# Turning q, k and u by DMA, masks on GpSimd too, and one written order for TensorE, in a fused attention and mixer kernel

## The chip, the cores and the metric

The kernel runs on one core of one Trainium2 chip. The metric is the time of one execution on the device in microseconds; the median of several runs is given. A core has five engines that run side by side: TensorE (PE in the profile) multiplies matrices and writes to PSUM, an accumulator memory of eight banks; VectorE (DVE) and ScalarE (ACT) read PSUM and work element by element; GpSimd (POOL) works on the main on-chip memory alone; SyncE (SP) only issues transfers. Transfers (DMAs) are issued from the queues of SP and POOL here, and 16 DMA engines carry them out.

## The reference

Inputs are q, k, v of 4 batches, 8 heads, 768 rows and 64 columns in float32. Attention keeps, for each row, the 128 latest keys and the first 4 (the "sinks"). Its result, put together over heads, is x of 768 x 512 for each batch, and a mixer follows:

```python
keep = is_sink | in_window
scores = np.where(keep, scale * q @ k.T, -1e9)
a = exp(scores - max) ; a = a / (sum(a) + 1e-09)
x = (a @ v) with the heads side by side        # 768 x 512 per batch
h = np.maximum(x.T @ w_tok1, 0.0) @ w_tok2     # over rows: 768 -> 256 -> 768
u = x + h.T
h2 = np.maximum(u @ w_ch1, 0.0) @ w_ch2        # over columns: 512 -> 1536 -> 512
return u + h2
```

## The kernel before

Heads go in pairs, four pairs to a batch: pair p belongs to batch p // 4, so there are 16. The two heads of a pair lie on the two halves of the 128 partitions once q and k are turned (columns of a head on partitions, rows along the free side), which is the form that TensorE needs for the scores.

**Loading.** Pairs 0 to 3 are loaded in float32 on SP's queue and cast to bfloat16 by an engine. Pairs 4 to 15, all v and all weights are loaded on POOL's queue with the cast in the DMA; each q or k takes two DMAs (one per head). Six buffers hold q and k of bfloat16 (`NQ`).

**Turning q and k.** `turn(p, n)` turns q or k of pairs 0 to 4 in a unit of its own. `transposed(p)` turns q and k of pairs 5 to 15: 24 transposes on TensorE into one of the two PSUM tiles that also serve the scores (`turned_bank`). Four copies (`evict`), on ACT or DVE, bring the halves of qT and kT to on-chip memory, two small ones take the sink columns of k (`sink_columns`), and a memset by DVE (`cleared`) puts zeros where the tile's next scores are not written.

**Scores.** `scores(p, g)` computes third g of a pair's scores, followed by an exp on ACT. From pair 4 on, the thirds 1 and 2 are computed by quarters: matmuls of 64 x 64 which use the four quarters of the array at a time and leave out blocks that are masked anyway. The third 0 is computed by halves, in matmuls of 64 x 128. For pairs 0 to 3 the mask is added on TensorE (`masked`), but for one third; for the others DVE multiplies the exp by a mask of ones and zeros (`mask`).

**Values and mixer.** `sink_values` and `values` multiply with v and add up in a PSUM bank for each head; DVE divides and writes x_sb. `mix_h` and `mix_u` are the mixer over rows, in two groups of 256 columns for each batch; `mix_u` ends in an add on DVE that makes u. `turned_u` turns u on TensorE for batches 1 to 3, in 48 small transposes (24 in one case); batch 0 has `transpose_u`. Then `v1` (relu(u @ w_ch1), 24 units of four matmuls for each batch) and `out_part` (24 units of three matmuls of 512 columns, six output tiles of 128 rows for each batch), an add of u on DVE and a store on SP. The last output tile of the last batch is cut into columns of 256, 128 and 128 (`out_columns`).

**PSUM.** Of the eight banks four form the two tiles for scores ("sc"), four are single banks ("mx") for all else.

**Order.** A class `Plan` runs while the program is built. It holds an estimate of when each engine is free, gives each operation to an engine, and appends it to that engine's program; on the chip each engine and each queue then runs its own list in that order, and waits where an operand isn't ready. `run` takes TensorE's units from three sources: `first` (pairs 0 to 3 and the row mixer of batch 0, in the order in which they can begin by the estimate), `main` (the column mixer) and `side` (attention and row mixer of the later batches). `MERGED` says behind how many units of `main` each unit of `side` comes. A `burst` is one unit of several pieces that use half of the array: it turns q and k of pair p + 1, computes the first third of pair p's scores and the sink values of pair p - 1; a second burst computes the two other thirds.

Of the kernel before, what the change touches and what calls it, by code (L numbers as in the profile page):

```python
# [16 lines left out]
def kernel(  # L17
# [13 lines left out]
    nc = tc.nc  # L31
# [15 lines left out]
    MERGED = (  # L47
# [5 lines left out]
    )  # L53
    NQ = 6
    MASKED_BY_PE = [(p, g) for p in range(NHP) for g in range(NT // 2) if (p, g) != (NHP - 1, 0)]
# [4 lines left out]
    att_pool = ctx.enter_context(tc.tile_pool(name="att", bufs=2))  # L60
# [3 lines left out]
    osb_pool = ctx.enter_context(tc.tile_pool(name="osb", bufs=3))  # L64

    psum = ctx.enter_context(tc.tile_pool(name="psum", bufs=1, space=bass.MemoryType.PSUM))
    TAGS = {"sc": 2, "mx": 4}

    given = {}

    sc = [psum.tile([P, 2, 2, 4, D], FP32, name=f"ps_sc{n}", tag=f"sc{n}", bufs=1) for n in range(TAGS["sc"])]

    def bank(tag, *shape, dtype=FP32, slot=None):

        n = given[tag].pop(0) if slot is None else slot
        if tag == "sc":
            return sc[n]
        return psum.tile([P, *shape], dtype, name=f"ps_{tag}", tag=f"{tag}{n}", bufs=1)
# [5 lines left out]
    def rows_of(pidx, n):  # L84

        b, hp = pairs[pidx]
        return (q, k)[n][b, 2 * hp:2 * hp + 2].rearrange("h (p j) d -> p h j d", j=NT)
# [67 lines left out]
    keep_warm(7, 0)  # L155
# [27 lines left out]
    NKB = 2  # L183
# [28 lines left out]
    x_sb = [singles.tile([P, NT, DM], BF16, name=f"x_sb{b}") for b in range(B)]  # L212
# [37 lines left out]
    class Plan:  # L250
        def __init__(self):
            self.free = {"PE": 0.0, "ACT": 0.0, "DVE": 0.0, "SP": 0.0, "POOL": 0.0}
            self.queue, self.landings = 0.0, []
            self.half = False
            self.pending = []
            self.held = {t: [()] * n for t, n in TAGS.items()}

# [9 lines left out]
        def slots(self, tag):  # L267

            free = []
            for n, readers in enumerate(self.held[tag]):  # L270
                if all(r.done is not None for r in readers):
                    free.append((max((r.done for r in readers), default=0.0), n))
            return sorted(free)

        def spare(self):
            return self.slots("mx")[0][1]

        def start_pe(self, op):
            t = self.ready(op)
            if t is None:  # L280
                return None
            for tag, banks in op.need.items():
                free = self.slots(tag)
                if len(free) < len(banks):
                    return None
                t = max(t, free[len(banks) - 1][0])
            return max(t, self.free["PE"])
# [23 lines left out]
        def commit_pe(self, op, t):  # L311
            for tag, banks in op.need.items():
                given[tag] = [n for _, n in self.slots(tag)[:len(banks)]]
                for n, readers in zip(given[tag], banks):
                    self.held[tag][n] = readers
# [6 lines left out]
        def run(self, first, main, side):  # L322

            first, main = [list(u) for u in first], list(main)
            order = [[int(n) for n in unit.split("/")] for unit in MERGED.split()]
            side, behind = [side[n] for n, _ in order], [n for _, n in order]
            placed = 0
            while any(first) or main or side or self.pending:
                o = self.other()
                tm = self.start_pe(main[0]) if main else None  # L330
                ts = self.start_pe(side[0]) if side else None
                pick = "side" if side and (not main or behind[0] <= placed) else "main"
                t = tm if pick == "main" else ts
                early = [(t, u) for u in first if u for t in [self.start_pe(u[0])] if t is not None]
                if early:
                    soonest = min([t for t, _ in early] + ([] if t is None else [t]))
                    stay = [(t, u) for t, u in early if self.half and u[0].half and t <= soonest + SWITCH]
                    te, u = next((e for e in stay + early if e[0] <= soonest + (SWITCH if e in stay else 40.0)), (None, None))
                    if u is not None and (o is None or o[0] > te):
                        self.commit_pe(u.pop(0), te)  # L340
                        continue
# [11 lines left out]
                if pick == "main":  # L353
                    placed += 1
                else:
                    behind.pop(0)
                self.commit_pe((main if pick == "main" else side).pop(0), t)
# [35 lines left out]

    QH = NT // 2

    def prepare(p):
# [21 lines left out]
        free = ([("sk", p - 2)] if p >= 2 else [], [("s", p - NKB)] if p >= NKB else [])  # L418
# [10 lines left out]
        tiles["kT", p] = kT  # L429
# [31 lines left out]
    def transposed(p):  # L461

        def run():
            ps = turned_bank(p)
            for n in range(2):
                for j in range(NT):
                    for x in range(2):
                        rows = ds(D * x, D)
                        in_order(nc.tensor.transpose(ps[:, x, n, j], bfs[p, n][rows, j], ident[rows, rows]))  # L469
                tiles["ps_" + "qk"[n], p] = [ps[:, x, n].rearrange("d j p -> d p j") for x in range(2)]  # L470

        then = [*done["qT", p], *done["kT", p], done["kTs", p]]
        then.append(cleared(p, then))
        return piece(
            350, run, [done["q_bf", p], done["k_bf", p]], {"sc": [then]}, then, [("tq", p), ("tk", p)],
        )

    def turned_bank(key):

        tiles["ps_turned", key] = bank("sc")  # L480
        t = tiles["ps_turned", key].bitcast(BF16).rearrange("d x n b c -> d x n (b c)")[:, :, :, 2 * D:8 * D]
        return t.rearrange("d x n (j p) -> d x n j p", j=NT)

    def cleared(key, readers):

        op = Op(
            {"DVE": 400.0}, lambda e: in_order(nc.vector.memset(tiles["ps_turned", key][0:D, :, :, 3], 0.0)), readers,
        )
        op.urgent = 2
        return op  # L490
# [22 lines left out]
    def scores(p, g):  # L513
# [28 lines left out]
        def run():  # L542
            if ("pT", p) not in tiles:
                tiles["pT", p] = pt_pool.tile([P, 2, NT, 2, P], BF16, name="pT")
            if not by_pe:
                tiles["ps_s", p, g] = bank("sc")
            (by_quarters if quarters else by_halves)(tiles["ps_s", p, g])
# [4 lines left out]
        def exp(e):  # L552
            in_order(nc.scalar.activation(  # L553
# [4 lines left out]
        def mask(e):  # L558
            pt = part(tiles["pT", p][:, :, ds(2 * g, 2)])
# [15 lines left out]
    def score_sinks(p):  # L575


        def run():
            pT_sink = pt_pool.tile([P, (NT - 2) * P], BF16, name="pT_sink")
            tiles["ps_sk", p] = bank("mx", (NT - 2) * P)  # L580
            for n in (p - 1, p):
                tiles["pT_sink", n] = pT_sink
# [8 lines left out]
        def exp(e):  # L591
            in_order(nc.scalar.activation(tiles["pT_sink", p], tiles["ps_sk", p], AF.Exp, scale=scale))
# [5 lines left out]
        return piece(225, run, deps, {"mx": [[x]]}, [x], [("sk", p - 1), ("sk", p)])  # L598

    def pv(p, half):  # L600
# [30 lines left out]
        n = Op({"DVE": 550.0}, norm, [r])  # L631
# [10 lines left out]
    def sink_values(p):  # L642
# [15 lines left out]
        for i in range(2):  # L658
# [11 lines left out]
            done["x", p, i] = Op({"DVE": 550.0}, norm, [done["r", p, i]])  # L670
# [19 lines left out]
    def sink_rows(p):  # L690
        def both(e):
            for i in range(2):
                r = D * i + ODD * (p % 2)
                copy(e, v_sinks[p % NHP][r:r + n_sink, i], vs[p][0:n_sink, i, 0])

        done["vs", p] = Op({"ACT": 440.0, "DVE": 400.0}, both, [done["v", p], done["pv", p - NHP]])
# [18 lines left out]

    def uT_half(b, ct, half):
        uT = tiles["mix", b][2]
        return uT.rearrange("c (k t p) -> c k t p", k=NC, t=NT)[:, ct, half * QH:(half + 1) * QH]

    def mix_h(b, g, t0, n):  # L720
        c0, cn = group(b, g)

        def run():
            if ("mix", b) not in tiles:
                tiles["mix", b] = (
                    mix_pool.tile([P, NTOK, DM], BF16, name="h1T"),
                    mix_pool.tile([P, NT * DM], BF16, name="u_sb"),
                    mix_pool.tile([P, NC * S], BF16, name="uT"),
                )
# [7 lines left out]

        w = n * cn
        op = Op(
            {"ACT": 190.0 + 0.78 * w, "DVE": 150.0 + 1.05 * w},  # L740
            lambda e: relu(e, tiles["mix", b][0][:, t0:t0 + n, c0:c0 + cn], tiles["ps_h", b, g, t0]),
# [367 lines left out]
```

## Time and profile before

| what | value |
|---|---|
| median of 3 runs | 207.51 us (207.47 to 207.58) |
| span of the profiled execution | 206.7 us |
| granted TensorE clock | 1.000 |
| v1 matmuls, 384 columns | 384, 66.3 us busy |
| output matmuls, 512 columns | 276 seen, 64.9 us busy |
| exp on ACT, 128 x 1024 | 32, 1,027 ns each |
| issue on POOL of a DMA of q or k | 48, about 823 ns each |
| store of an output tile, 256 KB, issue to landing | 2.0 us (median) |
| load of q, 96 KB, issue to landing | 7.0 us (median) |

The span is the time from the first to the last instruction of one profiled execution; the runs' times are of unprofiled ones and lie 0.8 us above it. Lengths of matmuls overlap, as a matmul begins before the one before it has left the array, so their sum is not the time that they take. "Idle before" of an engine tells what ended its wait. The chain follows the execution back from its end, at each step to what was waited for.

### The profile page before, as it was taken

To read this page: it belongs to the slowest core of one execution; us is meant where nothing else is said; L and a number is where in the kernel's file an instruction comes from. 1 tells how busy PE (TensorE), PEld (TensorE's weight loads), DVE (VectorE), ACT (ScalarE), POOL (GpSimd) and SP (SyncE) were. 2 spreads that over 40 slices of the span, in tenths; PEclk is the share of its full clock that TensorE was granted. 3 is DMA by queue.
4 is the path that set the end of the run, shared out by engine and by line. 5 is a ranking of instruction groups with operands and counts; after the bars stand their busy time and mean duration, and the time that the engine had idled before them with its cause. 6 is when DMAs were issued, how large, how long until landed. Compare 5 with 4: busy or idle time off the path is not lost.

```text
span 206.7 us, 5560 instructions
## 1 busy us (share of the span) xinstructions
PE 199.5 (97%) x2377; PEld 119.8 (58%) x2377; DVE 114.8 (56%) x263; ACT 119.0 (58%) x225; POOL 67.3 (33%) x86
## 2 busy tenths in 40 slices
PE   6798999999999999999999999999999999999994
PEld 2344795565565665666665555656655555565443
DVE  4687545649767777566675775784357252000222
ACT  4599666878744744888676443977562105773000
POOL 6099687696499984441000000000000000000000
PEclk9999999999999999999999999999999999999999
DMA  6999999999999999596001121100001212000223
GB/s 197 293 228 137 165 190 176 170 160 197 175 184 175 186 190 182 79 107 43 0 3 54 51 101 55 54 0 3 0 3 51 101 54 101 0 3 0 101 101 102
DMA packets 73223, 21.58 MB, mean 104 GB/s; under 512 B 63216, under 2 KB 70256, under 8 KB 73200
## 3 DMA queue, kind: packets, MB, share of 16 engines
q0 software_dynamic: 67232, 11.80, 72.7%
q1 hardware_dynamic: 5968, 9.45, 12.8%
q8 instruction: 18, 0.29, 0.6%
q14 instruction: 5, 0.04, 0.1%
HBM read 26.75 MB, written 6.29 MB: 160 GB/s over the span
## 4 chain that ended last, share of the span: by engine, by line
PE 86%; DMA 7%; DVE 2%; POOL 1%; ACT 1%; issue 0%; SPq 0%; POOLq 0%
PE ps_mx L121 78%; PE ps_sc L121 4%; DMA w_tok<-in_moe_w_tok_dram 4%; DMA v_sink_f<-in_v_dram 3%; PE ps_sc L469 2%; PE ps_mx L439 1%; POOL v_aug L114 1%; PE ps_mx L124 1%; SPq L200 0%; DVE u_sb L765 0%; POOL v_sink L130 0%; DVE qT L130 0%; PE ps_mx L451 0%; DVE kT L130 0%; DVE x_sb L664 0%
## 5 line engine op out<-in xcount | busy, mean ns | idle before, releaser
L121 PE MATMUL ps_mx<-w_ch,v1T 128*128 128x512 bf16 (+2 forms) x312 | 67.5, 363 | 0.0
L121 PE MATMUL ps_mx<-uT,w_ch 128*128 128x384 bf16 x384 | 66.3, 326 | 0.3 <-DVE recip L661 0.3
L553 ACT ACTIVATE pT<-ps_sc 128x1024 bf16<-128x1024 f32 (+1 forms) x48 | 44.5, 955 | 12.1 <-PE ps_sc L121 11.8
L121 PEld LDWEIGHTS <-w_ch 128*128 128x128 bf16 x384 | 36.2, 98 | 24.5 <-issue 1.5
L134 ACT ACTIVATE v1T<-ps_mx 128x384 bf16<-128x384 f32 x74 | 36.1, 493 | 16.5 <-PE ps_mx L121 16.0
L121 PEld LDWEIGHTS <-v1T 128*128 128x128 bf16 x312 | 28.2, 98 | 26.9 <-issue 0.7
L938 DVE TENSOR_TENSOR o_sb<-ps_mx,u_sb 128x512 f32<-128x512 f32 x23 | 15.9, 690 | 37.2 <-PE ps_mx L121 37.2
L121 PEld LDWEIGHTS <-w_tok 128*128 128x128 bf16 x192 | 18.4, 98 | 7.0 <-DMA w_tok<-in_moe_w_tok_dram 1.2
L106 POOL DMA_DIRECT2D q_bf<-in_q_dram x24 | 19.7, 824 | 4.6 <-DMA w_ch<-in_moe_w_ch_dram 2.0
L106 POOL DMA_DIRECT2D k_bf<-in_k_dram x24 | 19.6, 822 | 4.5 <-DMA w_ch<-in_moe_w_ch_dram 2.2
L114 POOL DMA_DIRECT2D v_aug<-in_v_dram x16 | 16.5, 1030 | 10.6 <-PE ps_mx L121 5.6
L765 DVE TENSOR_TENSOR u_sb<-ps_mx,x_sb 128x512 bf16<-128x512 f32 x20 | 13.2, 687 | 9.0 <-PE ps_mx L121 8.9
L136 DVE TENSOR_SCALAR v1T<-ps_mx 128x384 bf16<-128x384 f32 x22 | 12.2, 558 | 7.8 <-PE ps_mx L121 7.0
L121 PE MATMUL ps_mx<-v_aug,pT 128*128 128x65 bf16 x352 | 15.5, 194 | 0.0
L121 PEld LDWEIGHTS <-pT 128*128 128x128 bf16 x352 | 13.8, 97 | 2.7 <-issue 0.6
L121 PE MATMUL ps_sc<-qT,kT 64*64 64x192 bf16 (+3 forms) x288 | 15.0, 252 | 0.0
L561 DVE TENSOR_TENSOR pT<-pT,mask_main 128x1024 bf16<-128x1024 bf16 (+1 forms) x24 | 13.9, 618 | 0.0
L121 PE MATMUL ps_mx<-h1T,w_tok 128*128 128x256 bf16 x96 | 13.4, 272 | 0.0
L121 PE MATMUL ps_mx<-x_sb,w_tok 128*128 128x256 bf16 x96 | 12.0, 273 | 0.9 <-DMA w_tok<-in_moe_w_tok_dram 0.9
L130 DVE COPY qT<-ps_sc 128x384 bf16<-128x384 bf16 x11 | 6.1, 558 | 11.8 <-ACT qT L128 11.8
L664 DVE TENSOR_TENSOR x_sb<-ps_mx,recip 128x384 bf16<-128x384 f32 x22 | 11.6, 549 | 0.1
L128 ACT ACTIVATE kT<-ps_sc 128x384 bf16<-128x384 bf16 x16 | 7.3, 489 | 6.9 <-DVE qT L130 6.9
(74 smaller groups left out, 166.3 us busy)
## 6 DMA issues: line engine op xcount, KB each, us to landing
out_dram<-o_sb SPq DMA_DIRECT2D x23, 256.0 KB, 2.0
v_aug<-in_v_dram POOLq DMA_DIRECT2D x16, 192.0 KB, 7.0
w_ch<-in_moe_w_ch_dram POOLq DMA_DIRECT2D x8, 384.0 KB, 8.9
q_bf<-in_q_dram POOLq DMA_DIRECT2D x24, 96.0 KB, 7.0
k_bf<-in_k_dram POOLq DMA_DIRECT2D x24, 96.0 KB, 6.0
q_f<-in_q_dram SPq DMA_DIRECT2D x4, 384.0 KB, 5.9
k_f<-in_k_dram SPq DMA_DIRECT2D x4, 384.0 KB, 6.2
w_tok<-in_moe_w_tok_dram POOLq DMA_DIRECT2D x2, 384.0 KB, 8.5
```

What stands on the lines that cost most here:

```text
L106: in_order(nc.gpsimd.dma_start(out=out[:, h], in_=rows[:, h]))
L114: in_order(nc.gpsimd.dma_start(out=v_aug.rearrange("p i t d -> p (i t) d")[:, :, 0:D], in_=v[b].rearrange("h s d -> (h s) d")[2 * hp * S:2 ...
L121: in_order(nc.tensor.matmul(*args, skip_group_check=True, **kwargs))
L128: in_order(nc.scalar.activation(out, in_, AF.Copy))
L130: in_order({"DVE": nc.vector, "POOL": nc.gpsimd}[e].tensor_copy(out=out, in_=in_))
L134: in_order(nc.scalar.activation(out, in_, AF.Relu))
L136: in_order(nc.vector.tensor_scalar_max(out=out, in0=in_, scalar1=0.0))
L553: in_order(nc.scalar.activation(part(tiles["pT", p][:, :, ds(2 * g, 2)]), of_keys(tiles["ps_s", p, g])[:, :, 0:width(g)], AF.Exp, scale=scale,
L561: in_order(nc.vector.tensor_tensor(out=pt, in0=pt, in1=m, op=ALU.mult))
L664: in_order(nc.vector.tensor_tensor(out=x_sb[b][:, :, ds((2 * hp + i) * D, D)], in0=tiles["ps_o", p, i][:, :, 0:D], in1=tiles["recip", p, i ...
L765: in_order(nc.vector.tensor_tensor(out=u_part(b, g, s0, n), in0=tiles["ps_u", b, g, s0], in1=x_sb[b][:, s0:s0 + n, c0:c0 + cn], op=ALU.add,))
L938: in_order(nc.vector.tensor_tensor(out=o_sb.rearrange("p (g c) -> p g c", g=2), in1=u_rows(b, st), in0=tiles["ps_out", b, st].rearrange("p ...
```

## The change

In short: (1) q and k of pairs 8 to 15 (`BY_DMA = 2 * NHP`) are turned by DMAs on SP's queue, on-chip memory to on-chip memory, as one DMA for each q and k; their rows are loaded in another assignment to partitions (row j x 128 + p on partition p), and the sink columns of k are copied from kT. `kTb` and the pool of qT have three buffers in place of two. (2) u of batches 2 and 3 is turned by one DMA behind each `mix_u` (three for a group, six for a batch). (3) Copies of sink rows of v to `v_sinks` are DMAs on SP where they were copies of ACT. (4) The thirds 1 and 2 may have their mask from POOL, in four selects, where the plan gives it that. (5) `transposed`, now for pairs 5 to 7, takes two single banks; the memset `cleared` goes. (6) When the units of the first pairs and of batch 0's row mixer are all placed, the second tile of the scores also serves as two single banks; in that tile the thirds 1 and 2 are computed by halves, in the first tile by quarters. (7) `ORDERED` is the whole order of TensorE's units, by streams: s, m, t, o, h, g for the first pairs and batch 0, a for attention, k for the row mixer, c for v1 and x for output units of three matmuls. (8) The last output tile is whole; o_sb has two buffers for three, x_sb two for four. (9) Eight subtractions of blocks of w_ch2 on DVE are put in (`weight_sums`); they serve another way of multiplying (`products`), which `BY_SEVEN = ()` switches off.

```diff
-    MERGED = (
...
+    ORDERED = (
+        "t0-1 m0 s0 m1 s1 t2 m2 t3 s2 m3 s3 o0 m4 t4 s4 m5 t5 o1 s5 t6 m6 o2 s6 o3 m7 t7 s7 m8 s8 o4 m9 s9-10 g0 "
+        "s11 g1 m10 o5-6 s12 o7 g2 o8 a0 g3 a1 h0-1 g4-5 h2-4 g6 h5-6 a2 c0-2 g7 h7 c3 a3 c4-9 a4 c10-12 a5 "
+        "c13-14 a6-7 c15-18 a8-10 x0 c19-20 k0 a11 x1 k1 x2 c21-23 k2-3 x3 a12-14 x4-6 a15 x7-10 a16 x11 a17-18 "
+        "x12-14 k4 x15-16 k5-7 x17-19 a19 x20-23 c24 a20 c25-26 a21-22 c27-28 a23 c29-31 a24 c32-35 a25-26 c36-37 "
+        "a27 c38-39 k8 c40-41 a28 x24 a29 c42-43 a30 c44 k9 a31 c45 k10 x25 c46 k11 c47 x26 a32 x27 a33-34 x28 "
+        "a35 x29-30 k12 x31 a36 k13 a37-38 x32-33 k14 a39 x34-44 a40 x45-46 k15 x47 a41 c48-49 a42 c50 a43 c51-53 "
+        "k16 c54-55 k17 c56 a44-45 c57 a46 c58-59 k18 c60-62 a47 x48 c63-64 k19 c65 a48 c66 a49 c67-71 k20 x49-50 "
+        "k21 x51-55 k22-23 x56-67 c72 x68 c73 x69-70 c74 x71 c75-86 x72 c87-95 x73-95"
     )
+    SC_LATE = 1
+    BY_SEVEN = ()
+    BY_DMA = 2 * NHP
...
+        if pidx >= BY_DMA:
+            return rows.rearrange("h (j p) d -> p h j d", p=P)
...
+                    for n in range(2 * SC_LATE if self.late else 2 * NSC, 2 * NSC + NMX):
...
+        if p >= BY_DMA:
+            def turn(e, n):
+                if not n:
+                    tiles["qT", p] = att_pool.tile([P, S], BF16, name="qT2")
+                in_order(nc.sync.dma_start_transpose(
+                    out=(kT if n else tiles["qT", p]).rearrange("c (t p) -> c t p", t=NT),
+                    in_=bfs[p, n].rearrange("p t h d -> p (t h d)"),
+                ))
+
+            for n, name in enumerate(("q", "k")):
+                op = Op({"SP": 1500.0}, lambda e, n=n: turn(e, n), [done[name + "_bf", p], *free[n]], lag=4000.0)
...
+            done["kTs", p] = Op(
+                {"POOL": 300.0, "DVE": 300.0}, sinks_of, done["kT", p] + [("sk", p - NHP)],
+            )
...
+            (by_quarters if quarters and tiles["ps_s", p, g] is sc[0] else by_halves)(tiles["ps_s", p, g])
...
+            if e == "POOL":
+                for n in range(2):
+                    nk = 2 if n == 0 or g < NT // 2 - 1 else 1
+                    for i in range(2):
+                        pt = tiles["pT", p][:, i, 2 * g:2 * g + nk, n]
+                        in_order(nc.gpsimd.affine_select(
+                            out=pt, in_=pt, compare_op=ALU.is_ge, fill=0.0, base=-n,
+                            pattern=[[0, nk], [1 - 2 * n, P]], channel_multiplier=2 * n - 1,
+                        ))
+                return
...
+            if g:
+                then[-1].cost["POOL"] = 1700.0 if g < NT // 2 - 1 else 1450.0
...
-                copy(e, v_sinks[p % NHP][r:r + n_sink, i], vs[p][0:n_sink, i, 0])
+                in_order(nc.sync.dma_start(out=v_sinks[p % NHP][r:r + n_sink, i], in_=vs[p][0:n_sink, i, 0]))
...
+        if pairs[BY_DMA][0] <= b:
+            def turn(e):
+                in_order(nc.sync.dma_start_transpose(
+                    out=tiles["mix", b][2].rearrange("c (g t p) -> c g t p", g=2, p=P)[:, g, 2 * s0:2 * (s0 + n)],
+                    in_=u_part(b, g, s0, n).rearrange("p t c -> p (t c)"),
+                ))
+
+            then.append(Op({"SP": 1500.0}, turn, [op], lag=4000.0))
...
-            if b == B - 1 and st == NT - 1:
-                units += [out_columns(st, 0, 2 * P), out_columns(st, 2 * P, P), out_columns(st, 3 * P, P)]
-                continue
...
+                o_sb = tiles["o_sb", b, st] = osb_pool.tile([P, DM], FP32, name="o_sb", bufs=2)
...
+        for name, out, in0, in1, of in (
+            ("T1", t1, b12, lambda: b11, ()), ("T2", t2, b22, t1, ("T1",)),
+            ("T3", t3, b22, lambda: b12, ()), ("T4", t4, b21, t2, ("T2",)),
+        ):
...
+            queue((name, c), Op({"DVE": 85.0 + 0.53 * k * DM // 2}, run, loaded + [done[n, c] for n in of]))
...
+    for c in range(2):
+        weight_sums(c)
```

More of the change, by code (lines that the diff above doesn't have):

```diff
@@ L320, in commit_pe, with run @@
             self.pending.extend(op.then)
[L322 to L328, printed above, removed]
-                o = self.other()
[L330 to L340, printed above, removed]
-                        continue
+        def run(self, units, early):
+            early = len(early)
+            units = list(units)
+            while units or self.pending:
+                self.late = early == 0
+                o = self.other()
+                t = self.start_pe(units[0][1]) if units else None
                 if o is not None and (t is None or o[0] <= t):
@@ L392, in piece, with joined, run @@
         return op
+    def joined(*units):
+        def run():
+            for u in units:
+                u.fn()
+        need = {}
+        for u in units:
+            for f in u.then:
+                f.deps = [d for d in f.deps if d is not u]
+            for tag, banks in u.need.items():
+                need.setdefault(tag, []).extend(banks)
+        return unit(
+            sum(u.size for u in units), run, [d for u in units for d in u.deps], need,
+            [t for u in units for t in u.then], half=units[0].half,
+        )
     QH = NT // 2
@@ L463, in run @@
         def run():
-            ps = turned_bank(p)
+            ps = [bank("mx", 2, NT, D, dtype=BF16) for _ in range(2)]
             for n in range(2):
```

453 lines of the change are left out of this document (293 added, 160 removed), and 5 rows, old and new, of the table MERGED.

## The prediction

> **What bounds the kernel now.** I read the page's busy rows and slices first, then the chain that ended last, then a table of stages, and last the timeline around the steps that the change touches.
>
> ```profile
> PE 199.5 (97%) x2377; PEld 119.8 (58%) x2377; DVE 114.8 (56%) x263; ACT 119.0 (58%) x225; POOL 67.3 (33%) x86
> ...
> DMA  6999999999999999596001121100001212000223
> ...
> PE 86%; DMA 7%; DVE 2%; POOL 1%; ACT 1%; issue 0%; SPq 0%; POOLq 0%
> ```
>
> TensorE (PE) is busy nearly throughout and makes 86% of the chain; VectorE (DVE) and ScalarE (ACT) have over 40% free. The DMA engines are full up to slice 18 (93 us) and nearly idle later. Busy alone is no proof for a pipelined engine, so the stages (span; then PE, PEld, DVE, ACT, POOL busy; clock; DMA):
>
> ```profile
> 21.00:62.00 41.00, 40.55 (x509) 27.00 (x508) 26.01 (x61) 29.32 (x57) 30.50 (x38) 1.00 1.90 178
> 62.00:98.00 36.00, 35.96 (x556) 22.28 (x554) 24.98 (x57) 24.02 (x49) 22.51 (x27) 1.00 1.68 138
> 98.00:140.00 42.00, 42.00 (x587) 25.32 (x585) 29.44 (x62) 26.16 (x53) 0.00 (x0) 1.00 0.11 39
> 140.00:170.00 30.00, 30.00 (x268) 18.03 (x269) 15.04 (x29) 11.37 (x21) 0.00 (x0) 1.00 0.10 37
> 170.00:204.00 34.00, 33.76 (x250) 19.04 (x249) 5.72 (x11) 12.60 (x25) 0.00 (x0) 1.00 0.15 57
> ```
>
> From 21 us on PE idles about 0.5 us (0.45 in the first row, 0.04 in the second; the 0.24 of the last row is its end at 203.8). So from there the span is a sum of PE work: a PE instruction removed shortens it, and work on other engines costs nothing until PE waits for it. Before 21 us the chain is loads and casts; the first pairs keep their instructions, and the written order there (turn, mask, scores) is nearly that of the trace, so I put this stage at no change.
>
> **The change, part by part.** Its turns on PE are seen here (start, length, engine and line, shape):
>
> ```profile
> 103.00 0.35 PE L469 MATMUL ps_sc<-ident,q_bf 64*128 64x64 bf16 x12
> ...
> 103.18 0.34 PE L469 MATMUL ps_sc<-ident,k_bf 64*128 64x64 bf16 x12
> ...
> 103.36 0.38 PE L121 MATMUL ps_sc<-qT,kT 64*128 64x256 bf16 x4
> ...
> 103.58 0.28 PE L121 MATMUL ps_mx<-v_sink,pT_sink 64*128 64x65 bf16 x8
> ...
> 107.81 0.49 PE L121 MATMUL ps_sc<-qT,kT 64*64 64x192 bf16 x16
> ...
> 108.12 0.60 PE L439 MATMUL ps_mx<-ident,u_sb 64*64 64x64 bf16 x48
> ...
> 108.65 2.76 PE L121 MATMUL ps_mx<-w_ch,v1T 128*128 128x512 bf16 x12
> ```
>
> Lengths overlap in the pipeline, so I take start to start. **Turns of q and k**: 103.36 - 103.00 = 0.36 us a pair, eight pairs, -2.9 us. The chain gives each 0.46 by its modelled ends, -3.7; starts decide, so -2.9, with -3.7 kept for the range. **Turns of u**, four pieces (two batches, two groups): the chain has 0.44, 0.44, 0.35 and 0.51, together 1.74; by starts the first is 108.65 - 108.12 = 0.53. I take -1.8. Together -4.7.
>
> **Scores by halves.** In the second PSUM tile of the scores the later two thirds are now computed by halves. Four matmuls of 256 columns take 103.58 - 103.36 = 0.22, and the 16 by quarters 108.12 - 107.81 = 0.31. Both thirds by halves would be 0.22 + 0.75 x 0.22 = 0.385, so +0.075 for both; as the burst needs both tiles at once, one third changes: +0.04 in 12 pairs, +0.5 us, between 0.2 and 0.9.
>
> **The tail.** The last output tile is again one of 512 columns. Its PE time is equal (6,144 columns either way). Its add takes 690 ns (the 128x512 row) in place of the 0.29 of the chain's last line, +0.4; its 256 KB store lands in 2.0 us, the 64 KB one has no landing row (128 KB: 1.7), 0 to +0.3. I take +0.5.
>
> **Evictions and memsets that go.** Per pair four copies of 128x384 (489 ns on ACT, 558 on DVE), a memset of 272 ns, two v_sink copies of 253 ns; these were hidden under PE and their removal saves nothing. The same cover hides what DVE gains: eight subtractions for sums of w_ch2, which nothing reads here, of 128x768 like the 553 ns mask row: 4.4 us near 50 to 60 us, with DVE at 26 of 41 us. Without cover each costs 0.55.
>
> **The transposes on SP.** Nothing in the trace is one. 192 KB each for q and k, 128 KB each for u. Nearest rows: 256 KB stores land in 2.0 us, and the 96 KB q loads of the crowded stage in 7.0. For q and k both lie under cover: pair 8's last load is issued at 48.2 and lands some 6 us later (k_bf's row), near 54; its scores follow pair 9's turn at 69.9. That is 15 us for two transposes, 4 to 14 us. Pair 15 is loaded by 96 and needed after 139. For u the tightest place in the written order is k15 to c54: seven units x and c of 0.65 us (eight matmuls of 384 columns take 1.29 from 104.48 to 105.77, a unit has four), two of values of 0.35 (22 matmuls for both from 103.79 to 104.48), a burst of 0.5 (the 0.31 above and its sinks) and a mix_h of 1.3 (12 matmuls of 256 columns, half of a 0.22 pair each), together 7.0 us; behind u's eviction (0.69) a transpose of 2.0 fits, one of 7.0 misses by about 1 us, in one batch. That stage has a DMA share of 0.11, so it is nearest to the 2.0. I take 0 for the transposes, at most +2.
>
> **What queues behind them on SP**: the stores and the small v_sink copies (two a pair). o_sb has two buffers for three, so an add waits for the store two tiles back, holding a PSUM bank of PE. Two tiles of 12 matmuls are 5.2 us; add, issue and landing take 0.69 + 0.33 + 2.0, so 2.2 us of delay on SP is free. **On POOL**, masks queue among load issues (0.82 us each); the loads run 15 us ahead. A mask in four pieces of 256 columns, by the POOL selects of 128 columns (290 ns) and 512 (638), is some 1.6 us against DVE's 0.69; the exp pair (1.03 + 0.81) and this fit into the shortest cover (a15 to a17: five units of 0.65 and a burst of 0.5, 3.75 us) with little to spare. For all new waits I take +0.4, between -0.5 (the idle time now there) and +2.
>
> **Sum**: -4.7 + 0.5 + 0.5 + 0.4 = -3.3 us. Span 206.7 becomes 203.4. The shown median, 207.51, lies 0.8 above the span; with that, **204.2 us**. Its own range: the low ends (-5.4, +0.2, +0.4, -0.5) give 202.2, the high ends (-4.6, +0.9, +0.8, +2) give 206.6.
>
> **Rivals.** (a) *SP becomes the bound* (slower). If a transpose among the loads holds SP's queue until it lands, at the 7.0 us of a q load, a pair costs SP 14 us plus 1 for copies and stores. From 54 us, pairs 8, 9, 10 are turned by 69, 84 and 99; the scores now need them at about 70, 84 and 92.5 (just behind the turns at 69.9, 83.5 and 92.1). Pair 10 comes 6.5 us late; after 98 us SP catches up. 204.2 + 6.5 = **210.7**. It decides from a hold of about 6 us ((92.5 - 54) / 3, less 1, halved). For it: the DMA digits of 9 to slice 16. Against it: 96 KB loads are many packets under 512 B (63,216 of 73,223), and their 7.0 holds the queueing of their own kind.
> [...]
>
> (b) *Masks late on POOL* (slower). A mask behind one pair's load issues (4 x 0.82 + 1.02 = 4.3 us) ends 1.84 + 4.3 + 1.6 = 7.7 us after the scores where 3.75 is covered, 4 us late; PE then stands at the pair's values. One to two such pairs before the loads end at 95 us: **208 to 212**. For: POOL is busy 22.5 of 36 us there. Against: DVE has 11 us free in that row, and only masks that it can't take go to POOL. If none goes, the change does not do what it says there, at no cost.
>
> (c) *Banks* (gain given back). Turns of pairs 5 to 7 now take two mx banks beside two for the sink values, where they had a score tile. The evictions of such a turn ran from 44.86 to 47.06, 2.2 us; if half of it stalls PE, three pairs cost 3.3: **207.5**. For: the 0.28 us in which PE waited for recip at 48.1, behind these copies. Against: mx may now take free score banks too.
>
> **Chances.** Forecast 0.63, (a) 0.14, (b) 0.10, (c) 0.11 (spread about its time), another 0.02. A measurement of this kernel tells 0.2%, some 0.4 us, from no change. Faster: 0.63 and a third of (c), 0.67; same: 0.05; slower: (a), (b) and the rest, 0.28. The range 202.2 to 209.0 leaves out (a), most of (b) and a little below.
>
> **What would show it.** Right: no PE rows of L469's kind on q_bf or k_bf from pair 8 on, PE busy 4 to 5 us less, PE idle after 21 us still under 1.5 us, transposes on SP landing in 2 to 7 us, the last add at 690 ns. Wrong: PE's waits naming qT, kT or uT by DMA (a), a POOL mask (b), or ACT and DVE copies near 35 to 60 us (c); or stores spaced by SP. A start that does not reach the first mix_h by 21 us would refute my zero there.

## The result and the profile after

The changed kernel took **220.6 us** (median; runs 219.72, 220.4 and 220.8) against 207.55 for the kernel before on the same chip: ratio **1.062**, 95% interval 1.059 to 1.065. Forecast were 204.2 and a range of 202.2 to 209.0. Ratios, here and below, leave out disturbed executions, such as the one (687.08 us, span 685.3) in which the profile was first taken; the profile read here is of another execution of the same kernel (a_look, 221.21 us).

> The changed kernel as it is, for a profile. In the profile on hand TensorE ran every matmul 3.9 times slower than its columns ask for, from the first to the last (685.3 us), so it tells nothing of waits. Theory: the time of 220.6 us is made of new TensorE waits of 10 us or more in a few places, and of a lowered clock after them (granted clock 0.98 in the other runs). Rival: the waits are small (under 3 us) and TensorE's pace itself is lower over long stretches, as 5 us of the 13 would be at a mean clock of 0.976.

The page of a_look first: busy time by engine, PE's and DMA's slices and the granted clock, and the chain that ended last.

```profile
span 219.4 us, 4716 instructions
...
PE 201.8 (92%) x1945; PEld 115.3 (53%) x1945; DVE 105.8 (48%) x232; ACT 103.7 (47%) x178; POOL 69.8 (32%) x94
...
PE   6999988999995879955999999999999999999993
...
PEclk9999999999999699995899999999999999999999
DMA  6999999999999999999092457420230342100222
...
PE 56%; DMA 33%; POOL 5%; SPq 2%; issue 1%; DVE 1%; ACT 0%; POOLq 0%; DVEq 0%
```

A slice is now 5.5 us. PE's share of the chain fell from 86 to 56% and DMA's rose from 7 to 33%. Most of the loss is in few slices: 13 to 15 (66 to 82 us) and 18 and 19 (93 to 104 us). In three slices in or just behind these (14, 19 and 20) the granted clock falls too, which it does in no slice of the profile before. The DMA engines are full until about 104 us in place of 93, as 25,200 packets go through the hardware queue, SP's, in place of 5,968.

By stages (columns as in the prediction) most of PE's new idle time lies between 62 and 140 us: 6.7 and 3.4 us in stages that had 0.04 and none.

```profile
62.00:98.00 36.00, 29.28 (x346) 16.15 (x343) 16.80 (x41) 13.41 (x19) 21.15 (x25) 0.95 1.99 162
98.00:140.00 42.00, 38.60 (x356) 21.92 (x357) 21.82 (x44) 17.70 (x27) 3.26 (x9) 0.92 0.64 99
```

PE's waits in a_look (total, times, longest) name a copy of a few hundred bytes first:

```profile
PE ps_mx L143 <- DMA v_sink<-v_aug: 8.7, 3, 4.8
...
PE ps_mx L143 <- DVE o_sb L1142: 1.4, 1, 1.4
PE ps_mx L538 <- DMA k_bf<-in_k_dram: 0.9, 1, 0.9
```

The timeline of a_look shows the first of the two long ones (start, length, what; in brackets the idle time before it):

```profile
63.99 0.55 SPq L1148 DMA_DIRECT2D out_dram<-o_sb  x1
...
64.60 1.26 SPq L764 DMA_DIRECT2D v_sink<-v_aug  x2
...
68.27 0.39 PE L143 MATMUL ps_sc<-qT,kT 64*128 64x256 bf16 x4
...
72.29 0.58 PE L143 MATMUL ps_mx<-v_sink,pT_sink 64*128 64x65 bf16 x8 [3.63 <-DMA v_sink<-v_aug]
72.80 1.46 PE L143 MATMUL ps_mx<-w_ch,v1T 128*128 128x512 bf16 x3
```

The two DMAs are issued at 64.60 and 65.28. By the semaphore events in the trace, the last of a DMA taken as its landing, they land at 72.25 and 72.42, so 7.6 and 7.1 us after the start of their issue; PE needs the rows at 68.4 and goes on at 72.29. Then three matmuls of 512 columns take 1.46 us; at the full granted clock three take 0.81 (before, at 112.49; clock 1.00). The second wait is 4.8 us, at 96.0 (v_sink issued at 95.84 and 96.51, landed at 101.01 and 101.52), with half pace until 106.

From the starts of PE's matmuls I list each gap of over 0.32 us beyond the matmul's own time. After 20 us they are 12.3 us in a_look (9.2 by v_sink at 68.4, 96.0 and 101.05; 1.6 at 31.6 and 32.4, where the turns of pair 5 wait, mostly for its loads; 1.5 at 80.6 by an add into o_sb) and 0.4 in the kernel before. The matmuls at half pace behind the long waits cost 3.8 us. The tail from the last matmul's start to the end is 4.07 us, before 3.18. So of the 12.7 us between the spans (219.4 - 206.7), waits make +11.9, pace +3.8, the tail +0.9, which leaves **-3.9 for PE's work**, as a remainder. The expected gain is there, and the waits with the half pace behind them outweigh it four to one.

### The profile page after: what moved, and what is told of

Read it like the earlier page. It is cut to its first block, busy times and chain, and to the rows that moved or that the text cites. A ratio compares the mean times of both kernels' runs of the same rounds, so it can differ in the third digit from the quotient of the medians.

```text
span 685.3 us, 4697 instructions
## 1 busy us (share of the span) xinstructions
PE 669.2 (98%) x1926; PEld 258.2 (38%) x1945; DVE 108.9 (16%) x232; ACT 106.4 (16%) x178; POOL 69.7 (10%) x94
## 3 DMA queue, kind: packets, MB, share of 16 engines
q1 hardware_dynamic: 25200, 14.18, 7.6%
## 4 chain that ended last, share of the span: by engine, by line
PE 97%; issue 2%; DVE 1%
PE ps_mx L143 83%; PE ps_sc L143 12%; PE ps_mx L520 1%; PE ps_mx L146 1%; PE ps_mx L538 1%; PE ps_mx L508 0%; DVE x_sb L734 0%; DVE o_sb L1142 0%; DVE q_bf L152 0%; DVE kT L152 0%; DVE ones L170 0%; DVE recip L731 0%; DVE kTs L152 0%; PE ps_sc L538 0%
## 5 line engine op out<-in xcount | busy, mean ns | idle before, releaser
L143 PE MATMUL ps_mx<-w_ch,v1T 128*128 128x512 bf16 x272 | 233.5, 1098 | 8.6 <-issue 8.1
L143 PE MATMUL ps_mx<-uT,w_ch 128*128 128x384 bf16 x340 | 217.8, 894 | 0.0
L143 PEld LDWEIGHTS <-w_ch 128*128 128x128 bf16 x384 | 80.5, 214 | 139.1 <-issue 138.4
L143 PEld LDWEIGHTS <-v1T 128*128 128x128 bf16 x288 | 60.5, 214 | 145.9 <-issue 145.9
L143 PEld LDWEIGHTS <-pT 128*128 128x128 bf16 x352 | 40.8, 171 | 16.8 <-issue 14.5
L143 PE MATMUL ps_mx<-h1T,w_tok 128*128 128x256 bf16 x92 | 44.0, 685 | 0.0
L143 PE MATMUL ps_mx<-x_sb,w_tok 128*128 128x256 bf16 x96 | 41.3, 685 | 0.0
L143 PE MATMUL ps_mx<-v_aug,pT 128*128 128x65 bf16 x319 | 41.2, 337 | 0.0
L143 PE MATMUL ps_sc<-qT,kT 64*128 64x256 bf16 (+2 forms) x240 | 37.3, 494 | 1.5 <-DVE q_bf L152 0.8
L143 PE MATMUL ps_sc<-uT,w_ch 128*128 128x384 bf16 x44 | 29.2, 868 | 0.0
```

Of the source, the lines that this page charges most:

```text
L143: in_order(nc.tensor.matmul(*args, skip_group_check=True, **kwargs))
```

## The experiments

Runs without an interval are single times; the kernel before took 207.1 to 207.7 us beside them. Kernels of this family vary more than that one (mended_v1_order: 207.16 to 213.85 us in ten runs), so a difference of a few us between two single times proves little by itself, and I read the waits in the traces beside it.

**1. The copies of v's sink rows.**

```diff
# sinks_by_copy
-                in_order(nc.sync.dma_start(out=v_sinks[p % NHP][r:r + n_sink, i], in_=vs[p][0:n_sink, i, 0]))
+                copy(e, v_sinks[p % NHP][r:r + n_sink, i], vs[p][0:n_sink, i, 0])
-        done["vs", p] = Op({"SP": 200.0}, both, ..., lag=2200.0)
+        done["vs", p] = Op({"ACT": 440.0, "DVE": 400.0}, both, ...)
# sinks_act_queue: as changed, but nc.scalar.dma_start and {"ACT": 200.0}
# before_sink_dma: the kernel before, with the changed kernel's DMA and Op for these copies
```

> The changed kernel, but the sink rows of v are copied by ACT or DVE again, as before; the transposes stay on SP. Theory S (the small copies on SP land 5 to 8 us after their issue while the DMA engines are full, and TensorE waits for them): the waits of TensorE on v_sink (3.8, 4.9 and 0.5 us) go, and the slow clock behind the two long ones with them (some 3 us), so 221.2 falls to 208 to 211; what stays is 1.6 us near 32 us and 1.5 us for a store. Theory T (the DMA engines cannot carry the transposes beside the loads): a wait for qT, kT or uT takes the place, the time stays over 216.

> The changed kernel, but the small copies of sink rows are DMAs on ACT's queue. If they are late because they stand in SP's list and ring behind transposes and stores, they land within about 3 us and the time falls as with copies, to 208 to 212. If any small DMA is late beside the loads, the waits on v_sink stay over 5 us in all and the time over 215.

> The kernel before with one part of the change alone: the sink rows of v are copied by DMAs on SP, where only the stores stand beside them. Theory S1 (late because of transposes ahead of them on SP): under 1 us of waits on v_sink, 207 to 208.5 us. Theory S2 (late beside the loads whatever stands on SP): several us of waits on v_sink, over 211 us.

Measured: **212.74**, **214.94** and **207.15** us. With the copies back on ACT and DVE no wait of PE names v_sink, and 8.5 of the 13.8 us go. That is less than I had expected (208 to 211 us), because a wait of 2.8 us for an add into o_sb comes at 77 us, and one of 1.8 for pair 5's loads at 32. On ACT's queue the time lies between the two that I had expected. The DMAs are issued earlier there, yet those of 62.96 and 63.59 land at 70.10 and 70.81, 7.1 and 7.2 us later, and PE still waits for v_sink some 3 us in all. In the kernel before, the same DMAs on SP cost nothing: no wait of PE names v_sink. Those issued at 62.79 and 63.45 land at 67.34 and 68.04, after 4.6 us, and are needed only at 69.13. So two things work together: a list on SP in which the copies stand behind stores and transposes, and a landing of 5.0 to 7.6 us (a_look) beside loads and transposes. Behind the loads one lands in 1.6 us (issued 128.17, landed 129.75 in a_look, in a slice with a DMA digit of 5).

SP's waits in a_look show what the list stands at: transposes (L468) that wait for buffers which PE must free, and for loads; the copies (L764) wait for the load of v.

```profile
...
SPq L764 <- DMA v_aug<-in_v_dram: 30.5, 3, 18.0
SPq L468 <- PE ps_mx L143: 22.8, 4, 10.4
SPq L468 <- DMA q_bf<-in_q_dram: 15.5, 4, 11.6
```

Totals don't tell where such waits hurt. The three of the copies end by 42.7 us, and two of the four for PE, the longest among them, come after 99 us; PE waits for v_sink behind none of these. What made the second long wait is one transpose of q (first of the two L468 rows): it stood at the head of SP's list from 89.35 to 93.94 us, and behind it the copies went out at 95.84, just as PE needed them.

**2. What is left near 77 us.** All but after_lag9, which starts from the changed kernel, start from sinks_by_copy.

```diff
# copy_osb3
-  o_sb = ... osb_pool.tile([P, DM], FP32, name="o_sb", bufs=2)
+  o_sb = ... osb_pool.tile([P, DM], FP32, name="o_sb", bufs=3)
# copy_lag9, after_lag9: the landing that the plan assumes for a transpose of q or k
-  op = Op({"SP": 1500.0}, lambda e, n=n: turn(e, n), ..., lag=4000.0)
+  op = Op({"SP": 1500.0}, lambda e, n=n: turn(e, n), ..., lag=9000.0)
# copy_lag9_order: copy_lag9, and in ORDERED
-  g6 h5-6 a2 c0-2 g7 h7 c3 a3
+  g6 h5-6 g7 h7 c0-1 a2 c2-3 a3
# copy_lag9_osb3: the edits of copy_lag9 and copy_osb3
```

> Sink rows by ACT or DVE as in sinks_by_copy, and o_sb with three buffers in place of two. If an add waits for the store two tiles back, the 1.5 us wait on o_sb near 81 us goes: 1 to 2 us less than sinks_by_copy. If the store's landing is not what sets it, no difference beyond 0.5 us.

> sinks_by_copy with one number changed: the plan counts 9.0 us for a transpose of q or k to land, not 4.0 (7.8 us was seen beside the loads), so the copies of the sink columns out of kT stand later in DVE's and POOL's lists. Theory D (a copy of kT's sink columns waits at the head of DVE's list for a transpose, and the adds behind it hold TensorE's banks): the waits of 2.8 us near 77 us and 1.5 us near 94 us go, and with their slow clock 212.7 falls to 207 to 209. Theory E (the add waits for the store's landing or for u): the wait near 77 us stays, 211 or more.

> The changed kernel with only the plan's 9.0 us for a transpose of q or k; the sink rows stay DMAs on SP. Theory S: the waits on v_sink stay, the one near 80 us goes, 217 to 221. If the copies of kT's sink columns are behind the waits on v_sink too, the time falls below 213.

> copy_lag9, and in the written order the first burst that turns pair 5 (a2) moves behind the remaining u turns of batch 0 and two units of v1. If the load of k of pair 5 sets that place, the 2.2 us wait near 32 us goes or halves: 1 to 2.2 us less than copy_lag9, some 205 to 207.5. If another operand sets it, the same as copy_lag9.

> The changed kernel with the sink rows of v copied by the engines, with 9000 ns instead of 4000 planned for the transposes' landing, and with three o_sb buffers instead of two (each of the last two alone left the time at 213.0 and 213.4 us). Theory: the waits of TensorE near 72 and 77 us have two causes, each enough alone: VectorE's o_sb add stands behind a kTs copy that waits for a transpose, and it waits for a store that lands 5 to 8 us after its issue. With both mended the 1.5 and 3.3 us of copy_lag9 at 72.2 and 77.35 us go, with some of the slow clock behind them: 208.0 to 209.5 us. Rival: the add waits for something else that is late (the matmuls' own input or a third transfer): 211 us or more, with a new releaser named before the add.

Measured: **213.04**, **213.37**, **220.44**, **211.19** and **210.25** us. The first two took nothing away, where the theories gave copy_osb3 1 to 2 us and copy_lag9 some 4, and their timelines say why. With three buffers (copy_osb3), the add into o_sb stands on DVE behind a copy of the sink columns, which waits for its transpose; PE waits for the add:

```profile
78.19 0.60 DVE L152 COPY kTs<-kT 64x4 bf16<-64x4 bf16 x2 [5.18 <-DMA kT<-k_bf]
78.83 0.69 DVE L1142 TENSOR_TENSOR o_sb<-ps_mx,u_sb 128x512 f32<-128x512 f32 x1
...
79.58 0.60 PE L143 MATMUL ps_mx<-h1T,w_tok 128*128 128x256 bf16 x4 [3.45 <-DVE o_sb L1142]
```

With the later landing planned (copy_lag9), that copy comes at 74.43, but the add waits for the store two tiles back to free its buffer:

```profile
79.97 0.69 DVE L1142 TENSOR_TENSOR o_sb<-ps_mx,u_sb 128x512 f32<-128x512 f32 x1 [4.95 <-DMA out_dram<-o_sb]
...
80.72 0.60 PE L143 MATMUL ps_mx<-h1T,w_tok 128*128 128x256 bf16 x4 [3.09 <-DVE o_sb L1142]
```

Each cause alone is enough to hold the same add until 79 or 80 us, so neither edit shows by itself. Together (copy_lag9_osb3) the waits at 72 and 77 us are gone. I had expected 208.0 to 209.5; it missed because a new wait of 2.2 us came at 94.1, for sink columns that GpSimd copied late between load issues. In copy_lag9_order the wait for pair 5's loads near 32 us went and one of 1.7 us for the third quarter of w_ch1 came at 35.05: the changed kernel makes v1 in an order that needs it early. With that and the waits at 72 and 77 us its time stayed above the expected 205 to 207.5. After_lag9, at 220.44 us as expected, still waits 8.0 us for v_sink: the plan's number alone does nothing while v_sink is late.

**3. The transposes without anything that hangs on them.** The kernel before computes all as it did; the 16 transposes of q and k of pairs 8 to 15 are added, and nothing reads their results.

```diff
+        if p >= 2 * NHP:
+            def turn_unread(n):
+                t = att_pool.tile([P, S], BF16, name=("unread_q", "unread_k")[n], bufs=3)
+                in_order(nc.sync.dma_start_transpose(
+                    out=t.rearrange("c (t p) -> c t p", t=NT), in_=bfs[p, n].rearrange("p t h d -> p (t h d)"),
+                ))
+            for n, name in enumerate(("q", "k")):
+                plan.pending.append(Op({"SP": 1500.0}, lambda e, n=n: turn_unread(n), [done[name + "_bf", p]], lag=4000.0))
```

> The kernel before, unchanged in all it computes, with the change's DMA transposes of q and k for pairs 8 to 15 added on SP's queue (16 transposes of 128x768 bf16), written to tiles that nobody reads. It costs the transposes' share of the DMA engines by itself, without any step that needs their result. Theory: the transposes lengthen the loads (packets rise from 73,223 to about 88,000, the DMA engines stay full until 100 us or more in place of 93) and delay the stores that follow on the queue, but before's own pairs are far enough ahead: 207.0 to 208.5 us, and what the change lost came from steps that wait on late transfers at the head of a queue. Rival: full DMA engines alone set TensorE back, as loads of later pairs come late for before too: 210 us or more with TensorE waiting for loads, stores or v_aug after 60 us.

Measured: **207.5 us**, ratio 1.0007 (0.9992 to 1.0022). Its slices and packets, and the issue (ns, min/median/max) and landing of its eight transposes of k:

```profile
DMA  6999999999999999999999121100001212000223
...
DMA packets 86024, 24.74 MB, mean 120 GB/s; under 512 B 76016, under 2 KB 83056, under 8 KB 86000
```

```profile
L433 SPq DMA_TRANSPOSE unread_k<-k_bf x8: 1215/1304/2193, 58.4 to 108.0; - x8
...
DMA to landing us min/median/max: 5.0/7.8/8.7
```

The DMA engines are full for over 110 us, longer than in the changed kernel (104), and the time is that of before. So here full DMA engines do not set TensorE back by themselves; steps that need a transfer soon after its issue do. A transpose of k holds SP for 1.3 us and lands 7.8 us after its issue (medians).

But the transposes, which alone differ between the two kernels, make other transfers later: the stores issued between 58 and 97 us land 3.6 to 5.9 us after their issue in the kernel before and 7.0 to 9.8 in before_unread_turns (six each, by the same events). That fits the v_sink copies, 4.6 us in before_sink_dma and 5.0 to 7.6 beside transposes (a_look). From 108 us on, behind the last load's issue at 107.65, a transpose of q or k lands in 2.7 to 3.9 us and one of u in 2.4 to 3.5 (a_look).

**4. The gain with the waits mended.** Each kernel adds edits to copy_lag9_osb3; the first takes a2's place from copy_lag9_order.

```diff
# mended_v1_order: order as copy_lag9_order, and v1 as in the kernel before
-  for c in range(2):
-      for half in range(2):
-          units += [v1(j * NH + c * KC + n, half) for j in range(2) for n in range(KC)]
+  for f0 in range(0, NF, 3):
+      units += [v1(ft, half) for half in range(2) for ft in range(f0, f0 + 3)]
# mended_kts_act: and the sink columns of k from a transpose, copied by ACT alone
-  done["kTs", p] = Op({"POOL": 300.0, "DVE": 300.0}, sinks_of, ...)
+  done["kTs", p] = Op({"ACT": 440.0}, sinks_of, ...)
# mended_tail: and o_sb with bufs=5, the last tile by out_columns as in the kernel before
+  x[-4:] = [out_columns(NT - 1, 0, 2 * P), out_columns(NT - 1, 2 * P, P), out_columns(NT - 1, 3 * P, P)]
# mended_tail_order: and in ORDERED
-  c0-1 a2 c2-3 a3 c4-9
+  c0-1 a2 c2-5 a3 c6-9
```

> The kernel copy_lag9_osb3 with two more edits: the projections of pair 5 (a2) stand behind g7 h7 c0-1 in the written order, and the v1 units are made in the order of the kernel before (three ft of both halves at a time), so that the third quarter of w_ch1 is not needed early. All transposes by DMA, the u transposes and the shared banks stay. Theory: the work taken off TensorE is worth the 4.7 us of the prediction less its 0.5 for scores by halves and some of the tail, and all that the changed kernel lost on top were waits for late transfers; with the waits near 32 us (1.6 us), near 35 us (1.7) and near 77 us gone the time is 204 to 206.5 us, below the kernel before (207.1 to 207.7). Rival: a cost of the change remains that is no wait (more time per matmul beside the transposes, slower evictions, a longer end): 207.5 us or more with TensorE's waits after 20 us under 1.5 us in total.

> The kernel mended_v1_order with one edit: the kTs copies of the pairs turned by DMA run on ScalarE alone, in place of GpSimd or VectorE. In mended_v1_order TensorE still waits 1.6 us near 35.7 (pT of ScalarE), 1.5 us near 78.8 (an o_sb add that stands behind a kTs copy on VectorE, which waits 1.98 us for its transpose) and 2.0 us near 96 (a kTs copy on GpSimd, at 97.98). Theory: only the place of the copies makes the last two; without them and the half clock behind them the fastest runs come to 204.5 to 206.5 us, below the kernel before. Rival: the transposes themselves land too late for their pair beside the loads, 8 us after their issue, wherever the copy stands; the copy then holds ScalarE's exps or relus and the wait only changes its name: 207 us or more in the fastest runs, a wait of 1 us or more near 79 or 96 us released by ScalarE.

> The kernel mended_kts_act with five o_sb buffers in place of three (the add at 79.74 us still waited 2.12 us for a store that was issued at about 71.8 and landed 7.9 us later) and with the last tile of the last batch in columns of 256, 128 and 128, as the kernel before has it. Theory: TensorE's path is some 4 us shorter than before's, covered by waits and the tail alone; the 1.4 us at 78.9 go, and of the tail's 0.9 us (from the last matmul's start to the end: 4.07 us, before 3.18): fastest runs 204.3 to 205.7 us, median 205 to 206.5. Rival: other costs hold the time, and a wait taken away only opens the next: median 207 us or more.

> The kernel mended_tail with the written order a2 c2-5 a3 c6-9 in place of a2 c2-3 a3 c4-9, so that two more v1 units stand between the turns and projections of pair 5 and its scores, where TensorE waited 1.6 us for pT at 35.8 us (ScalarE had a qT, two kTs and two v1T evictions ahead of that exp). Theory: 0.6 to 1.6 us less than mended_tail, so a median of 204 to 205.7 us. Rival: the two v1 units bring two more evictions ahead of the exp, and the wait stays or grows: within 0.4 us of mended_tail, or slower.

| kernel | us, median of all runs (lowest to highest) | ratio to before, 95% interval |
|---|---|---|
| mended_v1_order | 209.5 (207.16 to 213.85) | 1.0066 (1.0027 to 1.0104) |
| mended_kts_act | 207.76 (206.53 to 211.14) | 1.0019 (0.9989 to 1.005) |
| mended_tail | 206.02 (205.88 to 207.02) | 0.994 (0.9919 to 0.9962) |
| mended_tail_order | **205.61** (205.17 to 207.15) | **0.9913** (0.988 to 0.9946) |

The first two missed what I expected: waits of 1.6 us near 36 and of 1.4 to 1.5 near 79 us remained. In mended_kts_act the wait at 96 us is gone, but the chain between 70 and 82 us still goes through a store, even with three buffers:

```profile
71.21 0.60 DVE pT L627
71.81 7.84 DMA out_dram<-o_sb
...
79.74 0.70 DVE o_sb L1142
...
80.49 0.38 PE ps_mx L143
```

A store issued at 71.81 lands 7.84 us later. Five buffers and the last tile in columns took 1.7 us off (207.76 to 206.02; the tail went from 4.07 to 3.43 us), and the median of mended_tail is as expected. Near 36 us ScalarE had five evictions ahead of an exp that PE waited for. With two more v1 units ahead of pair 5's scores that wait of 1.6 us is gone from the trace, and one of 0.56 stands at 41.1. The medians differ by 0.4 us, less than the expected 0.6 to 1.6, and the runs of the two kernels overlap. Mended_tail_order is faster than both kernels, 2.0 us (0.9%) below the one before. It keeps the transposes of q, k and u by DMA, the shared banks and the one written order. It gives up the copies of v's sink rows by DMA, the two buffers of o_sb, the whole last tile and the new order of v1. Its page:

```profile
PE 194.7 (96%) x1951; PEld 114.6 (56%) x1969; DVE 106.9 (53%) x234; ACT 109.7 (54%) x210; POOL 68.5 (34%) x86
...
PE   6799999999999999999999999999999999999993
```

PE's digits are 9 from slice 3 to the last but one, much as before, with 426 matmuls fewer in the trace (1,951 for 2,377). The span of this profile, 203.4 us, is 3.3 below that of before. Longer waits (0.56 us for 0.44) and tail (3.41 for 3.18) make +0.35, so by the spans PE does 3.6 us less. Of this 0.3 lies before the first mix_h, which begins at 20.53 us here and at 20.85 before, where the loads decide; that leaves 3.3 for PE's work. By the medians it is 2.0 + 0.35 = 2.3.

## Why the prediction was wrong

**The path and PE's work: right in kind.** The turns of q and k from pair 8 on and of u in two batches are gone from PE, and the forecast net of them was -4.7 + 0.5 = -4.2 us. Measured were -3.9 by the two spans in the changed kernel. In mended_tail_order PE takes 179.5 us from the first mix_h to the start of the last matmul; in three executions without the change (before, before_sink_dma, before_unread_turns) it takes 182.7, 182.8 and 183.3. With 0.1 us more of waits than before this makes -3.3. Where that stretch begins varies with the loads, 19.4 to 20.9 us in those three, so whole spans and times mix that in. I took the median to lie 0.8 above the span; single executions whose time and span are both known lie 1.8 apart (221.21 and 219.4; 207.78 and 206.0). So the 206.7 of the profile belonged to an execution of some 208.5 us, longer than any run shown. The forecast doesn't suffer by it, as it is the shown median less 3.3.

**The step that failed: "For all new waits I take +0.4, between -0.5 (the idle time now there) and +2."** They were +11.9 us, and the half pace behind them, which the sum did not have at all, another 3.8. Within this step:

- The two v_sink copies of a pair were taken as things that queue behind the transposes. Their own landing was never priced, though the matmuls of the sink values need it soon. It made 9.2 of the 11.9; undone, 8.5 us of time.
- What the transposes do to the landing of the transfers beside them was not in the sum: stores beside the loads went from 3.6 to 5.9 us to 7.0 to 9.8 by the transposes alone (before_unread_turns).
- For stores the landing was put at 2.0 us, the median of the whole trace before, where the row also gave a maximum of 5.3. Beside loads and transposes it was 5.3 to 8.3 in a_look, so the "2.2 us of delay" that two buffers leave free was gone. The place was named (an add that waits for the store two tiles back, holding a bank), and the size was wrong.
- The copies of the sink columns from kT were not priced. They wait at the head of DVE's or POOL's list for a transpose.
- "the written order there (turn, mask, scores) is nearly that of the trace" was said of the time before 21 us only. I didn't compare the order near 32 us. Pair 5's turns now stand so early that they begin at 32.2 and 33.4, just as its loads land, where the turn stood at 35.45 before: 1.6 us of waits.

**The transposes under cover: right, with a wrong size.** The bounds were 2.0 to 7.0 us for one. Beside the loads the runs show a median near 8 (5.0 to 8.7 for k in before_unread_turns); for u, behind the loads, 2.4 to 3.5 us, near the 2.0 that was taken. Pair 8's last load lands at 57.4 us in a_look (57.7 before) and not near 54. No wait of PE on the DMA of qT, kT or uT appears in a_look, as "15 us for two" had enough in it. SP was held for 1.2 to 1.5 us by each of the eight transposes of k in a_look.

**The tail**: +0.9 against +0.5; the add was 0.69 as forecast. **Before 21 us**: no change, right (first mix_h at 20.83 us, before 20.85).

**The rivals.** (a) had the side, and the mechanism failed: SP is not held until a transpose lands (1.3 us in before_unread_turns, against the 6 from which it decides), and before_unread_turns has the transposes without loss. What SP's list is held by is the wait of a transpose for its load or buffer, and what is late behind it is the small copy. Moving the copies to another queue did not make them land sooner: 7.1 and 7.2 us in sinks_act_queue, 7.6 and 7.1 in a_look. A transpose takes 7.8 us beside the loads (median of k, before_unread_turns); behind them it is 2.7 us for q or k at the least in a_look, of which SP's issue takes 1.2. (b) is void: a_look has all 37 masks on DVE and none on POOL, so the change does not do what it says there. (c) did not show in the changed kernel: no gap of over 0.32 us stands between 33.5 and 68.4 us.

## What to carry to other kernels

Before a copy moves from an engine with free time to a DMA, price its landing at the load of the DMA engines in that very stage, with the change's own new transfers counted in, and not at the median of the trace. Then look for the instruction that needs it next. What an in-order list waits for at its head delays all behind it (on SP a transpose from 89.35 to 93.94 us, and so the copies of 95.84), so a wait can have two causes that are each enough alone: undo both before you drop either theory. Taking work off the critical engine gains only what the new waits leave of it, so list these waits, with the half pace that may follow them.

## What the runs showed of the hardware that I had not expected

- **Half pace after a wait.** Behind the wait of 4.8 us in a_look, thirteen matmuls of 384 columns start 0.32 us apart in place of 0.16. Behind the 3.6 us, matmuls of 512 start 0.43 apart in place of 0.216, and the 22 of 65 columns that follow 0.055 in place of 0.030. A row behind the second long wait, and a_look in stretches (columns as in the prediction; the granted clock is the last but two):

```profile
101.89 1.46 PE L143 MATMUL ps_sc<-uT,w_ch 128*128 128x384 bf16 x4
```

```profile
71.88:75.30 3.42, 3.01 (x34) 2.02 (x35) 0.84 (x3) 0.00 (x0) 2.38 (x3) 0.50 2.01 156
75.30:99.19 23.89, 19.62 (x210) 10.87 (x207) 12.07 (x27) 9.10 (x14) 12.97 (x16) 1.00 2.03 169
99.19:106.02 6.83, 4.69 (x21) 2.30 (x22) 1.46 (x3) 0.56 (x2) 0.80 (x2) 0.50 0.97 113
```

  So the granted clock was 0.50 for 3.42 us around the end of the wait of 3.6 us and for 6.83 us around that of 4.8, and 1.00 between them. In the other traces the clock falls to half for 3.41 us behind waits of 1.8 us (sinks_by_copy), 2.0 (mended_v1_order) and 2.2 (copy_lag9_osb3), each with a mean granted clock of 0.992, and not at all behind one of 2.9 (copy_lag9_order, 1.00 from 62 to 98 us). So here a wait of some 2 us was followed by up to 1.7 us more (half of the 3.41, an estimate), or by nothing. What decides between the two was not shown.
- **A few hundred bytes landed as late as 192 KB** while the DMA engines were full (DMA share 1.87 to 1.99 from 62 to 98 us): 5.0 to 7.6 us for v_sink (0.5 KB) in a_look, 7.8 for a transpose of k (median, before_unread_turns), 7.8 for a store of 256 KB (mended_kts_act, issued at 71.81). Behind the loads it was 1.6 for v_sink (a_look, issued at 128.17) and 2.0 for a store (median of 23 before, 17 of them issued from 110 us on, at DMA shares of 0.10 to 0.15).
- **Transposes made the transfers beside them later.** Stores among the loads took 3.6 to 5.9 us before and 7.0 to 9.8 with 16 unread transposes added (before_unread_turns).
